# A search that counts against thresholds: the offsets read from PSUM, and the running sum as a fifth column of the digit instruction

## The chip, the cores and the metric

The kernel runs on one core of a Trainium2 chip. The core has five engines with a queue each: PE (TensorE, the matrix products), DVE (VectorE), ACT (ScalarE), POOL (GpSimd) and SP (SyncE, here the queue that starts most DMAs). Each engine works its queue in order; semaphores hold an instruction back until what it needs is there. The metric is the device time of one execution in microseconds, lower is better.

## The reference

An attention part, a mixture of experts, and a second MLP, one after the other:

```python
x = attention(x, state)                       # 4352 tokens of 512 numbers
logits = x @ w_gate                           # 8 experts
order = np.argsort(-logits.flatten())
for idx in order:                             # greedy, best logit first
    tok, e = idx // 8, idx % 8
    if assigned[tok] >= 0 or counts[e] >= 544:
        continue
    assigned[tok] = e
    counts[e] += 1
for e in range(8):                            # each expert has 544 tokens
    h = np.maximum(x[assigned == e] @ w1[e], 0.0)
    out[assigned == e] = h @ w2[e]
h = out @ w_in                                # second MLP
out = np.maximum(0.01 * h, h) @ w_out
```

## The kernel before

It has three stages. `prologue` (0 to about 121 us) does the attention, the logits and the first of seven searches. `experts` (121 to 637 us) runs the eight experts one after the other, in the order in which they fill up, and beside them the other six searches. `mlp2` (to the end) is the second MLP.

**A search** replaces the greedy loop: it finds the expert that fills next, closes it, and leaves its tokens. Its core is `cutoff`, called twice a search (the high 16 bits of the logits, then the low 16): for each expert the 544th largest of 272 numbers in each partition's row `V`, over the rows that belong to that expert. It takes 7 steps. In a step four thresholds are counted: three by DVE (`jD`, line 211, 272 numbers each, `V` minus a running sum, compared with an offset, the count going into `cnt`), the fourth by ACT (`jA`, line 207, with a `bias` that DVE makes on line 200, and a small copy into `cnt`, line 208). PE adds the counts of all rows (`pc`, line 221), and DVE turns them into the next digit (`js`, line 224, whose accumulator output is `acc`). Then DVE's next step begins. Two small instructions behind the counts carry the running sum on: `T` (line 214) and `P` (line 218, the next step's four offsets with `T` added or taken away). At the end one more addition makes the result (`r_hi`, `r_lo`, line 227). So the chain of a step goes DVE, PE, DVE, and one search has 14 of them, and a tail on both engines; `slots` then turns the tokens into gather indices (`u1`, `u2`, `PL`, `rd` on DVE, `pr` on PE, lines 334 to 363).

**An expert** is two products on PE: the first (`pm`, line 872, 192 matmuls in 16 groups of 12) and the second (line 890, 192 matmuls in 8 groups of 24). Every factor is split into a high and a low part, so each group runs three times over its sums. ACT takes each group out of PSUM (lines 878 and 897), and the splits go to ACT (high part) and to POOL or DVE (low part, line 712): weights are `unit`, the hidden layer is `h`. The tokens of the next expert are gathered by POOL's indirect DMAs (`rows`), transposed on PE (`pt`, line 830) and split on ACT and DVE (`xt`, lines 833 and 837). The accumulators `pm` rotate through four PSUM buffers.

**What sets the order.** The program is written out by a small planner. It walks through the matmuls of `ffn`, adds up modelled time, and inserts side work when its time has come: search pieces, slots, weight splits, token transposes. `cutoff` is a generator; each `yield` says how long DVE is expected to take until the next count product, `g.dstep(k)`: 1.95 for k below 2, 2.35 for 2, 2.45 above. So PE's queue holds `pc` at a fixed place among the expert's matmuls: where PE comes to it before the counts are there, PE stands still, since its queue is in order. Experts are numbered 0 to 7 here by their turn; expert k+1 can start only when search k+1 and its slots are done.

These lines are the ones that the prediction's steps touch most:

```python
nc.vector.scalar_tensor_tensor(jD, V, acc, P[:, t:t + 1].to_broadcast([128, 272]), op0=OP.subtract,
                               op1=OP.is_ge, accum_out=cnt[:, t:t + 1])
...
nc.vector.scalar_tensor_tensor(js, pc, float(CAP), C(f"step_{nm}{i}"), op0=OP.is_ge, op1=OP.mult,
                               accum_out=acc)
```

Of the kernel before, what the change touches and what calls it, by code (L numbers as in the profile page):

```python
# [14 lines left out]
OP = mybir.AluOpType  # L15
# [13 lines left out]
MIN_HI = 3.4332275390625e-05  # the high word of 2**-126, read as a float32  # L29
# [4 lines left out]
def _layout_consts():  # L34
# [20 lines left out]
    add("sgn2", np.broadcast_to([1, 1, -1, -1], (128, 4)))  # L55
    add("sgn3", np.broadcast_to([1, 1, 1, -1], (128, 4)))
    add("iota8", np.broadcast_to(np.arange(8), (128, 8)))
    for nm, unit in (("hi", 65536.0), ("lo", 1.0)):
        for i in range(7):
            st = unit * 5.0 ** (6 - i)  # L60
            add(f"step_{nm}{i}", np.broadcast_to([st] * 4, (128, 4)))
            for nd in (2, 3):
                o = [(j + 1) * st if j < nd else 0.5 * unit - (j + 1) * st for j in range(4)]
                add(f"off{nd}_{nm}{i}", np.broadcast_to(o, (128, 4)))
# [29 lines left out]
def setup_select(g):  # L94
# [19 lines left out]
    g.PL = cp.tile([128, 2, 36], F16, name="PL")  # L114
    g.opn = cp.tile([128, E], F32, name="opn")


def load_consts(g, pool):
# [6 lines left out]
    def c(name):  # L125
# [7 lines left out]
        lambda: nc.gpsimd.memset(g.zero, 0.0),  # L133
        lambda: nc.gpsimd.memset(g.opn, 1.0),
        lambda: nc.gpsimd.memset(g.asg, 0.0),
# [1150 lines left out]
```

## Time and profile before

| what | value |
|---|---|
| median of 3 runs | 1423.05 us (1416.94 to 1424.54) |
| the profiled execution's span | 1423.3 us |
| PE busy | 1324.9 us, 93% of the span |
| DVE busy | 737.8 us, 52% |
| ACT, POOL busy | 567.3 us, 505.2 us |
| experts 0 to 7, first matmul to last | about 133 to 637 us |
| second MLP | about 637 to 1423 us |

[...] A matmul's row is longer than the distance to the next one, since matmuls overlap, so PE's idle time is better read from the gaps before a group of instructions than from its busy share.

### The profile page before, as it was taken

The numbers are of one execution on the slowest core, as the hardware profiler recorded it, in microseconds if no ns is written. First come the engines' busy times: TensorE is split into PE (matmuls) and PEld (weight loads), VectorE is DVE, ScalarE is ACT, GpSimd is POOL, SyncE is SP. The second block draws the span as 40 slices with busy tenths as digits, with TensorE's granted clock in tenths as the row PEclk, the third lists the DMA queues.
The fourth block names the chain that finished last, engine by engine and source line by source line (L and its number), as shares of the span: only waits on it lengthen the run. The fifth ranks groups of instructions, "written<-read, shape, count | busy, mean of one in ns | idle before, by whom it ended". The sixth has DMA issues, their size and how long they took to land.

```text
span 1423.3 us, 21798 instructions
## 1 busy us (share of the span) xinstructions
PE 1324.9 (93%) x8145; PEld 1123.0 (79%) x8145; DVE 737.8 (52%) x2071; ACT 567.3 (40%) x1309; POOL 505.2 (35%) x515
## 2 busy tenths in 40 slices
PE   9986678889898999989989999999999999999997
PEld 5564678889888999987668888888888888888886
DVE  6888998998888978557762121121211212112221
ACT  6765645566565646442332222222222222222222
POOL 2303655645546456354543122131221312212121
PEclk9997989999999999999999999999999999999999
DMA  8445050513223377554220000000000000000000
GB/s 344 182 163 210 30 157 26 177 65 123 97 85 125 103 233 247 195 175 138 75 103 30 30 30 30 1 30 30 30 30 1 30 22 30 8 1 30 0 30 15
DMA packets 58746, 123.29 MB, mean 87 GB/s; under 512 B 14992, under 2 KB 24208, under 8 KB 56720
## 3 DMA queue, kind: packets, MB, share of 16 engines
q1 hardware_dynamic: 49504, 102.78, 21.0%
q0 software_dynamic: 5536, 17.83, 3.7%
q10 hardware_dynamic: 3600, 1.29, 0.4%
q8 instruction: 64, 1.05, 0.3%
q14 instruction: 42, 0.34, 0.1%
HBM read 90.94 MB, written 30.93 MB: 86 GB/s over the span
## 4 chain that ended last, share of the span: by engine, by line
PE 70%; DVE 21%; issue 3%; DMA 3%; ACT 3%; POOL 0%; SPq 0%; ACTq 0%; DVEq 0%; POOLq 0%
PE po L1164 24%; PE ph L1147 24%; PE pm L890 7%; PE pm L872 7%; DVE jD L211 6%; PE px L589 2%; DVE bias L200 2%; DVE ot L1015 1%; PE ps L462 1%; DVE P L218 1%; DVE ot L1014 1%; DVE xt L837 1%; DMA rows<-xs,idall 1%; DVE unit L712 1%; DVE T L214 1%
## 5 line engine op out<-in xcount | busy, mean ns | idle before, releaser
L1164 PE MATMUL po<-unit,gt 128*128 128x512 f32 x1632 | 404.4, 396 | 4.9 <-POOL gt L712 4.0
L1164 PEld LDWEIGHTS po<-unit,gt 128*128 128x128 f32 x1632 | 305.5, 188 | 78.5 <-POOL gt L712 6.2
L1151 DVE TENSOR_TENSOR g<-ph,g 128x512 f32<-128x512 f32 (+1 forms) x144 | 95.3, 661 | 511.8 <-ACT g L1150 511.8
L712 POOL TENSOR_TENSOR gt<-g,gt 128x512 fp32r<-128x512 f32 (+1 forms) x80 | 101.9, 1273 | 419.7 <-ACT gt L708 386.9
L1150 ACT ACTIVATE g<-ph 128x512 f32<-128x512 f32 (+1 forms) x144 | 82.4, 572 | 400.4 <-PE ph L1147 400.4
L1147 PE MATMUL ph<-xt,unit 128*128 128x512 f32 (+1 forms) x960 | 215.9, 374 | 8.9 <-ACT unit L708 5.3
L890 PE MATMUL pm<-h,unit 128*128 128x288 f32 (+1 forms) x1536 | 219.6, 301 | 0.0
L872 PE MATMUL pm<-xt,unit 128*128 128x288 f32 (+1 forms) x1536 | 214.4, 296 | 4.3 <-DVE xt L837 2.4
L890 PEld LDWEIGHTS pm<-h,unit 128*128 128x128 f32 x1536 | 207.7, 199 | 0.1
L1147 PEld LDWEIGHTS ph<-xt,unit 128*128 128x128 f32 x960 | 171.8, 191 | 44.1 <-ACT unit L708 5.9
L872 PEld LDWEIGHTS pm<-xt,unit 128*128 128x128 f32 x1536 | 201.7, 193 | 5.3 <-DVE xt L837 2.8
L1147 PE MATMUL ph<-xt_b,unit 128*128 128x512 f32 x768 | 188.4, 394 | 0.0
L1147 PEld LDWEIGHTS ph<-xt_b,unit 128*128 128x128 f32 x768 | 144.0, 188 | 34.2
L712 POOL TENSOR_TENSOR unit<-raw,unit 128x512 fp32r<-128x512 f32 x97 | 128.8, 1340 | 109.9 <-ACT unit L708 109.2
L712 POOL TENSOR_TENSOR h<-h,h 128x288 fp32r<-128x288 f32 (+1 forms) x128 | 109.3, 861 | 88.4 <-ACT h L708 87.3
L211 DVE SCALAR_TENSOR_TENSOR jD<-V,acc,P 128x272 bf16<-128x272 f32 x252 | 139.0, 599 | 0.0
L708 ACT ACTIVATE gt<-g 128x512 fp32r<-128x512 f32 (+1 forms) x144 | 87.6, 608 | 104.8 <-DVE g L1151 104.8
L708 ACT ACTIVATE unit<-raw 128x512 fp32r<-128x512 f32 x144 | 88.2, 620 | 37.3 <-DMA raw<-wf 18.7
L207 ACT ACTIVATE jA<-V,bias 128x272 bf16<-128x272 f32 x84 | 43.8, 521 | 87.8 <-DVE bias L200 86.9
L712 DVE TENSOR_TENSOR gt<-g,gt 128x512 fp32r<-128x512 f32 (+1 forms) x64 | 42.2, 659 | 42.9 <-ACT gt L708 40.0
L878 ACT ACTIVATE h<-pm 128x288 f32<-128x288 f32 (+1 forms) x128 | 49.5, 386 | 35.4 <-PE pm L872 30.1
L712 DVE TENSOR_TENSOR unit<-raw,unit 128x512 fp32r<-128x512 f32 x47 | 39.5, 847 | 40.0 <-ACT unit L708 37.0
(212 smaller groups left out, 1240.1 us busy)
## 6 DMA issues: line engine op xcount, KB each, us to landing
raw<-in_w_dram SPq DMA_DIRECT2D x64, 512.0 KB, 4.3
unit<-in_x_dram SPq DMA_DIRECT2D x8, 1024.0 KB, 12.0
xs<-raw SPq DMA_DIRECT2D x16, 512.0 KB, 2.6
x<-xo SPq DMA_DIRECT2D x64, 128.0 KB, 2.7
raw<-in_win_dram SPq DMA_DIRECT2D x16, 512.0 KB, 3.7
raw<-in_wout_dram SPq DMA_DIRECT2D x16, 512.0 KB, 3.3
raw<-x SPq DMA_DIRECT2D x16, 512.0 KB, 4.4
unit<-in_xT_dram SPq DMA_DIRECT2D x7, 1024.0 KB, 9.9
```

The source lines that it names most:

```text
L200: nc.vector.scalar_tensor_tensor(bias, acc.to_broadcast([128, 4 - nd]), -1.0, P[:, nd:4], op0=OP.mult, op1=OP.add)
L207: nc.scalar.activation(jA, V, AF.Sign, bias=bias[:, t - nd:t - nd + 1], accum_out=cs[:, t - nd:t - nd + 1])
L211: nc.vector.scalar_tensor_tensor(jD, V, acc, P[:, t:t + 1].to_broadcast([128, 272]), op0=OP.subtract, op1=OP.is_ge, accum_out=cnt[:, t:t + 1])
L708: nc.scalar.activation(hi, src, AF.Copy)
L712: e.tensor_tensor(lo, src, hi.bitcast(F32), op=OP.subtract)
L872: nc.tensor.matmul(pm, w[:, a, c, wc], xt[k][:, b, c, o], start=(n == 0), stop=(n == 11))
L878: nc.scalar.activation(h32, pm, AF.Relu)
L890: nc.tensor.matmul(pm, w[:, a, c % 4, 128 * m:128 * m + 128], hs[half][:, b, c, :], start=(n == 0), stop=(n == 23))
L1147: nc.tensor.matmul(ph[:, :n], w[:, a, c, wc], xt[:, b, c, :n], start=(i == 0), stop=(i == 11))
L1150: nc.scalar.activation(g32[:, :n], ph[:, :n], AF.Copy, scale=0.01)
L1151: nc.vector.tensor_tensor(g32[:, :n], ph[:, :n], g32[:, :n], op=OP.max)
L1164: nc.tensor.matmul(pos[gi][t], gt[:, a, 128 * t:128 * t + 128], w[:, b, f % 4, :], start=(f == 0 and a + b == 0), stop=(f == NF - 1 and a ...
```

## The change

The offsets of all 14 steps become one constant row, `offs`, with the sign already in it, and do not depend on the running sum any more. `setup_select` makes a small table `stp` with a row of five columns for each step: four times the step's size, and the running sum. The digit instruction reads five columns: PE's product has five as well, because `cnt` has a fifth column that always holds 100, so the fifth comparison is always true, and the accumulator output is the old sum plus the new digit. It is written straight into the next row of `stp`. So `T`, `P` and the closing addition are gone. The counts on DVE take the sum as a pointer scalar (as before `acc`) and the offset as the broadcast second tensor; in the first search that offset lies in SBUF, in the six searches beside the experts it lies in PSUM: `g.offp`, copied there once at the start of `experts`. `bias` is now a `tensor_scalar` with one tensor input. To make room for `offp` among the eight PSUM banks, the accumulators `pm` rotate through three buffers, not four. The planner's `g.dstep` is 2.15 for all searches. Comments and docstrings are gone, which moves line numbers.

```diff
-    T, acc, P = g.zero, g.zero, C(f"off{nd}_{nm}0")
+    T = None
     for i in range(7):
-        cnt = cp.tile([128, 4], F16, name="cnt", bufs=2)
-        if i:
-            nc.vector.scalar_tensor_tensor(bias, acc.to_broadcast([128, 4 - nd]), -1.0, P[:, nd:4], op0=OP.mult,
-                                           op1=OP.add)
+        n = i if nm == "hi" else 7 + i
+        cnt = g.cnts[n % 2]
+        off = C("offs")[:, 4 * n:4 * n + 4]
+        offv = off if g.offp is None else g.offp[:, 4 * n:4 * n + 4]
+        if T is not None:
+            nc.vector.tensor_scalar(bias, off[:, ND:4], T, None, op0=OP.add)
...
-            nc.vector.scalar_tensor_tensor(jD, V, acc, P[:, t:t + 1].to_broadcast([128, 272]), op0=OP.subtract,
+            nc.vector.scalar_tensor_tensor(jD, V, g.zero if T is None else T,
+                                           offv[:, t:t + 1].to_broadcast([128, 272]), op0=OP.subtract,
                                            op1=OP.is_ge, accum_out=cnt[:, t:t + 1])
-        T2 = cp.tile([128, 1], F32, name="T", bufs=3)
-        nc.vector.tensor_tensor(T2, T, acc, op=OP.add)
-        T = T2
-        if i < 6:
-            P = cp.tile([128, 4], F32, name="P", bufs=2)
-            nc.vector.scalar_tensor_tensor(P, C(f"sgn{nd}"), T, C(f"off{nd}_{nm}{i + 1}"), op0=OP.mult, op1=OP.add)
...
-        nc.vector.scalar_tensor_tensor(js, pc, float(CAP), C(f"step_{nm}{i}"), op0=OP.is_ge, op1=OP.mult,
-                                       accum_out=acc)
-    r = cp.tile([128, 1], F32, name=f"r_{nm}", bufs=2)
-    nc.vector.tensor_tensor(r, T, acc, op=OP.add)
+        T = g.stp[:, n + 1, 4:5] if i < 6 else cp.tile([128, 1], F32, name=f"r_{nm}", bufs=2)
+        nc.vector.scalar_tensor_tensor(js, pc, float(CAP), g.stp[:, n, :], op0=OP.is_ge, op1=OP.mult,
+                                       accum_out=T)
...
-                pm = g.psa.tile([128, HMAX], F32, name="pm", tag="mm", bufs=4)[:, :H]
+                pm = g.psa.tile([128, HMAX], F32, name="pm", tag="mm", bufs=3)[:, :H]
...
-        g.dstep = lambda k: 1.95 if k < 2 else 2.35 if k < 3 else 2.45
+        g.dstep = lambda k: 2.15
...
+            g.offp = g.psa.tile([128, 56], F32, name="offp")
+            nc.vector.tensor_copy(g.offp, g.C("offs"))
```

Three places show what this does to the queues. The first is DVE's queue in a step of the search beside expert 0 (low half). Before:

```order
L224 SCALAR_TENSOR_TENSOR js,acc<-pc,cst 128x4
L200 SCALAR_TENSOR_TENSOR bias<-acc,P 128x1
L211 SCALAR_TENSOR_TENSOR jD_2532,cnt<-V_2416,acc,P 128x272
L211 SCALAR_TENSOR_TENSOR jD_2534,cnt<-V_2416,acc,P 128x272
L211 SCALAR_TENSOR_TENSOR jD_2536,cnt<-V_2416,acc,P 128x272
L214 TENSOR_TENSOR T<-T,acc 128x1
L218 SCALAR_TENSOR_TENSOR P<-cst,T 128x4
L224 SCALAR_TENSOR_TENSOR js,acc<-pc,cst 128x4
```

and now:

```order
L225 SCALAR_TENSOR_TENSOR js,stp<-pc,stp 128x5
L206 TENSOR_SCALAR bias<-cst,stp 128x1
L217 SCALAR_TENSOR_TENSOR jD_2423,cnt_111<-V_2316,stp,offp 128x272
L217 SCALAR_TENSOR_TENSOR jD_2425,cnt_111<-V_2316,stp,offp 128x272
L217 SCALAR_TENSOR_TENSOR jD_2427,cnt_111<-V_2316,stp,offp 128x272
L225 SCALAR_TENSOR_TENSOR js,stp<-pc,stp 128x5
```

Between two `js` stood six instructions, each with two tensor inputs in SBUF. Four are left: `bias` with one tensor input, and three counts with one input in SBUF (`V`) and one in PSUM (`offp`).

The second is PE's queue in the last steps of the search beside experts 2 and 3, where the first product of expert 3 runs. Before:

```order
L221 MATMUL pc<-cnt,m_104 128x4
L872 MATMUL pm<-xt,unit 128x256 x24
L221 LDWEIGHTS m_104
L221 MATMUL pc<-cnt,m_104 128x4
L872 MATMUL pm<-xt,unit 128x256 x22
L221 LDWEIGHTS m_104
L221 MATMUL pc<-cnt,m_104 128x4
L872 MATMUL pm<-xt,unit 128x256 x2
L872 MATMUL pm<-xt,unit 128x288 x18
L221 LDWEIGHTS m_104
```

and now:

```order
L222 MATMUL pc<-cnt_111,m_104 128x5
L871 MATMUL pm<-xt,unit 128x256 x21
L222 LDWEIGHTS m_104
L222 MATMUL pc<-cnt_110,m_104 128x5
L871 MATMUL pm<-xt,unit 128x256 x19
L222 LDWEIGHTS m_104
L222 MATMUL pc<-cnt_111,m_104 128x5
L871 MATMUL pm<-xt,unit 128x256 x10
```

Between two count products `pc` (`m_104` is their constant matrix) stood 20 to 24 matmuls of the expert; now 19 to 21 stand there.

The third is PE's queue where expert 0 ends (line 890 before, 889 now) and expert 1 starts (872, 871), with the token transposes `pt` of expert 1. Before, from the second of its transposes on:

```order
L830 MATMUL pt_3265<-ident,rows 128x128 x4
L890 MATMUL pm<-h_2499,unit 128x288 x7
L221 LDWEIGHTS m_104
L221 MATMUL pc<-cnt,m_104 128x4
L890 MATMUL pm<-h_2499,unit 128x288 x12
L872 MATMUL pm<-xt,unit 128x256 x3
L830 MATMUL pt_3328<-ident,rows 128x128 x4
L872 MATMUL pm<-xt,unit 128x256 x10
L221 LDWEIGHTS m_104
```

and now, from the first on:

```order
L829 MATMUL pt_3070<-ident,rows 128x128 x4
L889 MATMUL pm<-h_2357,unit 128x288 x4
L222 LDWEIGHTS m_104
L222 MATMUL pc<-cnt_110,m_104 128x5
L889 MATMUL pm<-h_2357,unit 128x288 x2
L829 MATMUL pt_3110<-ident,rows 128x128 x4
L871 MATMUL pm<-xt,unit 128x256 x28
L222 LDWEIGHTS m_104
L222 MATMUL pc<-cnt_111,m_104 128x5
L871 MATMUL pm<-xt,unit 128x256 x13
```

The second transpose of expert 1 stood 19 matmuls ahead of the expert's first one; now it stands right in front of it.

## Rows read from the trace of the kernel before

**Rows 1.** The page: busy us of each engine (share); PE's granted clock in tenths, 40 slices.

```profile
PE 1324.9 (93%) x8145; PEld 1123.0 (79%) x8145; DVE 737.8 (52%) x2071; ACT 567.3 (40%) x1309; POOL 505.2 (35%) x515
...
PEclk9997989999999999999999999999999999999999
```

**Rows 2.** Busy time by stretch: experts 0, 1, 4, 7; expert 0's first product.

```profile
core 0: us, PE busy (x) PEld busy (x) DVE busy (x) ACT busy (x) POOL busy (x), PEclk, DMA share, GB/s
...
133.00:218.00 85.00, 64.32 (x441) 59.88 (x442) 76.29 (x268) 44.17 (x126) 47.91 (x45) 0.87 0.31 96
218.00:283.00 65.00, 56.33 (x447) 53.02 (x446) 59.18 (x219) 38.09 (x109) 40.26 (x38) 1.00 0.33 105
...
411.00:472.00 61.00, 56.77 (x443) 54.77 (x442) 53.44 (x215) 37.22 (x105) 33.18 (x35) 0.94 0.35 107
...
586.00:637.00 51.00, 48.65 (x387) 48.22 (x385) 29.41 (x32) 23.57 (x55) 28.57 (x25) 1.00 0.66 209
...
133.00:180.00 47.00, 34.03 (x216) 30.95 (x217) 43.37 (x148) 28.33 (x83) 27.92 (x27) 0.87 0.15 50
```

**Rows 3.** Groups (busy us, mean ns, idle before): whole run; expert 0; a wait at 126-133.

```profile
L200 DVE SCALAR_TENSOR_TENSOR bias<-acc,P 128x1 f32<-128x1 f32 x84 | 38.9, 463 | 5.6
...
L221 PE MATMUL pc<-cnt,m 128*128 128x4 f16 x98 | 17.6, 179 | 38.3 <-DVE jD L211 32.8 <-ACT h L708 2.3 <-ACT unit L708 1.6
L351 PE MATMUL pr<-PL,u 128*128 128x36 f16 x40 | 4.1, 182 | 8.9 <-DVE PL L346 8.9
...
L221 PE MATMUL pc<-cnt,m 128*128 128x4 f16 x20 | 3.7, 184 | 22.1 <-DVE jD L211 21.9 <-ACT unit L708 0.2
...
PE pc L221 <- DVE jD L211: 3.0, 1, 3.0
```

**Rows 4.** DVE by line: duration in ns min/median/max, first and last start.

```profile
L211 DVE SCALAR_TENSOR_TENSOR jD<-V,acc,P x252: 486/495/7095, 84.2 to 484.9; 128x272 bf16<-128x272 f32 x126
...
L200 DVE SCALAR_TENSOR_TENSOR bias<-acc,P x84: 158/160/2941, 84.2 to 483.2; 128x1 f32<-128x1 f32 x84
...
L214 DVE TENSOR_TENSOR T<-T,acc x84: 143/152/1243, 85.5 to 485.3; 128x1 f32<-128x1 f32 x84
...
L262 DVE TENSOR_TENSOR V<-pm,KH x7: 440/441/442, 81.8 to 433.0; 128x272 f32<-128x272 f32 x7
...
L251 DVE TENSOR_TENSOR mk<-L,mg x7: 429/433/441, 79.1 to 432.0; 128x272 bf16<-128x272 f32 x7
...
L837 DVE TENSOR_TENSOR xt<-pt,xt x40: 277/683/691, 128.0 to 579.5; 128x512 fp32r<-128x512 f32 x32, 128x128 fp32r<-128x128 f32 x8
...
L340 DVE TENSOR_SCALAR ce<-tot,ce x8: 212/214/215, 117.9 to 498.7; 128x1 f32<-128x1 f16 x8
...
L346 DVE TENSOR_SCALAR PL<-sc,ce x8: 229/236/1235, 118.7 to 499.8; 128x34 f16<-128x34 f32 x8
...
L358 DVE TENSOR_TENSOR rd<-rr,cst x8: 329/1188/1457, 120.0 to 501.4; 128x170 f32<-128x170 f32 x8
```

**Rows 5.** Timeline, expert 0's second product: start, us, engine, instruction.

```profile
202.45 7.09 DVE L211 SCALAR_TENSOR_TENSOR jD<-V,acc,P 128x272 bf16<-128x272 f32 x1
...
203.08 6.16 POOL L712 TENSOR_TENSOR unit<-raw,unit 128x512 fp32r<-128x512 f32 x5
...
210.46 0.19 PE L221 MATMUL pc<-cnt,m 128*128 128x4 f16 x1 [6.01 <-DVE jD L211]
```

**Rows 6.** Timeline, first search: two digit instructions on DVE; POOL's first work behind it.

```profile
107.71 0.16 DVE L224 SCALAR_TENSOR_TENSOR js<-pc,cst 128x4 f32<-128x4 f32 x1
...
109.69 0.16 DVE L224 SCALAR_TENSOR_TENSOR js<-pc,cst 128x4 f32<-128x4 f32 x1
...
121.06 0.18 POOL L365 COPY idt<-idall 32x1 int32<-32x1 int32 x1 [54.07 <-DVE idall L363]
```

**Rows 7.** Timeline of PE where expert 7 starts.

```profile
586.13 5.77 PE L872 MATMUL pm<-xt,unit 128*128 128x256 f32 x48
593.84 4.43 PE L872 MATMUL pm<-xt,unit 128*128 128x256 f32 x35 [1.94 <-ACT h L878]
```

More of the change, by code (lines that the diff above doesn't have):

```diff
@@ L28 @@
 BIG = 1.0e36
+ND = 3
 MIN_HI = 3.4332275390625e-05
@@ L54, in _layout_consts @@
     add("erev", 8 - p % 8)
-    add("sgn2", np.broadcast_to([1, 1, -1, -1], (128, 4)))
-    add("sgn3", np.broadcast_to([1, 1, 1, -1], (128, 4)))
     add("iota8", np.broadcast_to(np.arange(8), (128, 8)))
-    for nm, unit in (("hi", 65536.0), ("lo", 1.0)):
+    steps, offs = [], []
+    for unit in (65536.0, 1.0):
         for i in range(7):
             st = unit * 5.0 ** (6 - i)
[L61 to L64, printed above, removed]
+            steps += [st] * 4 + [0.0]
+            offs += [(j + 1) * st - (0.0 if j < ND else 0.5 * unit) for j in range(4)]
+    add("steps", np.broadcast_to(steps, (128, 70)))
+    add("offs", np.broadcast_to(offs, (128, 56)))
     _CONST["_n"] = (0, sum(c.shape[1] for c in cols))
@@ L114, in setup_select @@
     g.PL = cp.tile([128, 2, 36], F16, name="PL")
+    g.stp = cp.tile([128, 14, 5], F32, name="stp")
+    g.cnts = [cp.tile([128, 5], F16, name=f"cnt{i}") for i in range(2)]
     g.opn = cp.tile([128, E], F32, name="opn")
@@ L132, in load_consts @@
         lambda: nc.gpsimd.memset(g.ones, 1.0),
-        lambda: nc.gpsimd.memset(g.zero, 0.0),
+        lambda: [nc.gpsimd.memset(g.zero, 0.0)] + [nc.gpsimd.memset(c, 100.0) for c in g.cnts],
         lambda: nc.gpsimd.memset(g.opn, 1.0),
-        lambda: nc.gpsimd.memset(g.asg, 0.0),
+        lambda: [nc.gpsimd.memset(g.asg, 0.0), nc.gpsimd.tensor_copy(g.stp.rearrange("p i t -> p (i t)"), C("steps"))],
         lambda: nc.gpsimd.memset(g.neg16, -1.0),
@@ L188, in keys, with cutoff @@
     return [turn, copy, sign, order, low, high, low_out, high_out]
-def cutoff(g, k, nm, V, nd):
+def cutoff(g, k, nm, V):
     nc, cp, C = g.nc, g.cp, g.C
-    T, acc, P = g.zero, g.zero, C(f"off{nd}_{nm}0")
+    T = None
     for i in range(7):
-        cnt = cp.tile([128, 4], F16, name="cnt", bufs=2)
-        if i:
-            bias = cp.tile([128, 2], F32, name="bias", bufs=2)[:, :4 - nd]
-            nc.vector.scalar_tensor_tensor(bias, acc.to_broadcast([128, 4 - nd]), -1.0, P[:, nd:4], op0=OP.mult,
-                                           op1=OP.add)
+        n = i if nm == "hi" else 7 + i
[3 more added lines that the diff above has]
+        if T is not None:
+            bias = cp.tile([128, 2], F32, name="bias", bufs=2)[:, :4 - ND]
+            nc.vector.tensor_scalar(bias, off[:, ND:4], T, None, op0=OP.add)
@@ L202, in cutoff @@
         else:
-            bias = P[:, nd:4]
+            bias = off[:, ND:4]
         cs = cp.tile([128, 2], F32, name="cs", bufs=2)
-        for t in range(nd, 4):
+        for t in range(ND, 4):
             jA = cp.tile([128, 272], BF16, name="jA")
-            nc.scalar.activation(jA, V, AF.Sign, bias=bias[:, t - nd:t - nd + 1], accum_out=cs[:, t - nd:t - nd + 1])
-        nc.scalar.activation(cnt[:, nd:4], cs[:, :4 - nd], AF.Copy, scale=0.5, bias=136.0)
-        for t in range(nd):
+            nc.scalar.activation(jA, V, AF.Sign, bias=bias[:, t - ND:t - ND + 1], scale=-1.0,
+                                 accum_out=cs[:, t - ND:t - ND + 1])
@@ L210, in cutoff @@
+        nc.scalar.activation(cnt[:, ND:4], cs[:, :4 - ND], AF.Copy, scale=-0.5, bias=136.0)
+        for t in range(ND):
             jD = cp.tile([128, 272], BF16, name=f"jD{t}")
-            nc.vector.scalar_tensor_tensor(jD, V, acc, P[:, t:t + 1].to_broadcast([128, 272]), op0=OP.subtract,
+            nc.vector.scalar_tensor_tensor(jD, V, g.zero if T is None else T,
+                                           offv[:, t:t + 1].to_broadcast([128, 272]), op0=OP.subtract,
                                            op1=OP.is_ge, accum_out=cnt[:, t:t + 1])
-        T2 = cp.tile([128, 1], F32, name="T", bufs=3)
@@ L231, in first_max @@
+    g.res[nm] = T
 def first_max(g):
@@ L233, in first_max, with search @@
     nc.vector.tensor_reduce(g.mg, g.L, axis=AX.X, op=OP.max)
-def search(g, k, nd=3):
+def search(g, k):
     nc, cp, C = g.nc, g.cp, g.C
@@ L262, in search @@
     nc.vector.tensor_tensor(V1, pm, g.KH, op=OP.mult)
-    yield from cutoff(g, k, "hi", V1, nd)
+    yield from cutoff(g, k, "hi", V1)
     Hs = g.res["hi"]
@@ L266, in search @@
     nc.vector.scalar_tensor_tensor(V2, V1, Hs, g.KL, op0=OP.subtract, op1=OP.add)
-    yield from cutoff(g, k, "lo", V2, nd)
+    yield from cutoff(g, k, "lo", V2)
     Lo = g.res["lo"]
@@ L689, in prologue @@
         bg = xread()
-        se = search(g, 0, g.nd0)
+        se = search(g, 0)
         next(bg)
@@ L884, in ffn @@
             for m in range(4):
-                pm = g.psa.tile([128, HMAX], F32, name="pm", tag="mm", bufs=4)[:, :H]
+                pm = g.psa.tile([128, HMAX], F32, name="pm", tag="mm", bufs=3)[:, :H]
                 n = 0
@@ L1213, in moe_kernel @@
         setup_select(g)
-        g.nd0 = 3
+        g.offp = None
         g.gate0 = 4
```

6 lines of the change are left out of this document (2 added, 4 removed).

## The prediction

> **What bounds the kernel now.** I read the page first, then busy time by expert, then what PE waits for, then DVE's durations by line. PE is busy for 93% of the span [rows 1], so a gain must come from gaps on PE or from its clock. Those are in the experts. Expert 7, which has no search beside it, takes 51 us; experts 1 and 4 take 65 and 61, and expert 0 takes 85 [rows 2]. Some of the difference is work (token transposes, count products), but the largest gap is at `pc`: PE stands still for 38.3 us in front of the 98 count products, 22.1 of it in expert 0, and 3.0 in the opening [rows 3], which leaves 13.2 for experts 1 to 5. The releaser is nearly always `jD`, the last count on DVE.
>
> Why DVE is late is seen in its durations. The counts take 495 ns in the middle case and up to 7095; `bias` 160 and up to 2941; `T` 152 and 1243 [rows 4], and `P` is alike. Work of a fixed size should not spread like that. The worst count ran from 202.45 for 7.09 us, and beside it POOL did five splits back to back, 6.16 us; the count ended when they did, and PE waited 6.01 us [rows 5]. All four kinds read two tensors from SBUF. Instructions of the same engine with one tensor in PSUM do not spread: `V` 440 to 442 ns in 7, and `xt` with a middle of 683 and an end of 691 [rows 4]. So a DVE instruction with two SBUF inputs waits for POOL's splits, and one with a PSUM input does not. In the first search, before which and beside which POOL had nothing to do for 54 us, a step takes 1.98 us [rows 6].
>
> **Durations of the new step.** `T` and `P` lay behind the counts and beside the round trip through PE; where nothing stalls they cost nothing, and removing them gives nothing. The counts keep their form except for the PSUM input: `V` with PSUM takes 441 ns and `mk` with two SBUF inputs 433 [rows 4], so I add 0.01 us for each of three. `bias` becomes a `tensor_scalar` with a pointer; `ce` has that form, 214 ns against 160 [rows 4], 0.05 us more. So 1.98 becomes 2.06 us, with or without POOL at work. PE's queue now has 19 to 21 matmuls between two `pc`; 48 took 5.77 us [rows 7], 0.12 each, so 2.3 to 2.5 us, and about the same where they are wider and fewer. DVE is ready before PE arrives, with some 0.25 us to spare.
>
> **Opening** (126 to 133 us). The 3.0 us wait hangs on one `bias` that took 2.94 us. Of it 0.5 is left, since DVE still needs 2.06 us there: **-2.5**.
>
> **Expert 0, first product.** 47 us now, of which ACT is busy 28.3, POOL 27.9 [rows 2], and the 192 matmuls at 0.12 to 0.13 us need 24. With the waits of this half (22.1 less the one of 6.01 [rows 5] and, estimated, one more in the second product) gone, PE would need 32 plus what the opening steps with their token splits still cost, some 3. The three engines then want nearly the same time and feed each other, so I take 35: **-12**.
>
> **Expert 0, second product.** 38 us now; the waits of about 7 go for the most part, DVE's steps still meet `PL`, `u2` and `rd` of the slots, which keep their stalls (`rd` 329 to 1457, `PL` 229 to 1235 [rows 4]). **-6**.
>
> **Experts 1 to 5.** Of 13.2 us at `pc` I leave 7. In each search two steps still hold a slot instruction that waits for POOL: `rd` with about 0.9 us over its shortest, `PL` and `u2` with one us together, and the spacing between two `pc` is now shorter than the 20 to 24 matmuls of before. **-6**. PE also waits 8.9 us for `PL` in front of `pr` [rows 3]. `PL` stands in DVE's queue behind the stalled counts, `T` and `P` of that step; without those it comes on time in about two of three cases, since its own stall stays: **-6**.
>
> **The clock.** PE's granted clock was 0.87 over expert 0 and 0.94 over expert 4, against 1.00 in experts 1 and 7 [rows 2]. It is at the lower of its two levels for 12% of expert 4, so 3.7 us are lost there; experts 2 to 5 together lose perhaps 10. The low stretches come behind gaps of PE. With half of the gaps gone I take half: **-5** (expert 0's share is in its own sums).
>
> **What it costs.** Three accumulators: where expert 7 starts, PE ran four groups (48 matmuls) and then stood 1.94 us until ACT took the first one out [rows 7]. With three buffers it stops 12 matmuls earlier and goes on at the same time, so 1.44 us more; a place or two like it: **+2.5**. Token transposes: the second one of expert 1 now stands right in front of its first matmul. ACT and DVE must split it first, and DVE's split alone is 0.68 us [rows 4]: **+2**. Prologue: 12 steps with a dearer `bias`, less two additions: **+0.3**. The copy of `offp` falls where DVE waits for weights.
>
> Sum: -2.5 - 12 - 6 - 6 - 6 - 5 + 2.5 + 2 + 0.3 = -32.7. The profiled span is 1423.3 us and the median of the runs 1423.05, so the two stand alike, and I forecast **1391 us**. Behind expert 7 nothing changes: the second MLP starts when the experts end.
>
> **Rivals.** *Bias still waits.* `PL` is a `tensor_scalar` with one SBUF input, and it does spread, 229 to 1235 ns [rows 4]. If the new `bias` did so too, some waits would stay: its mean of 463 ns [rows 3] is 0.3 over its shortest, in 72 steps 22 us of DVE time, of which steps with 0.25 us to spare pass on about half: +11, **1402**. Against it stands `ce`, of exactly the new form with one element in a partition, 212 to 215 in 8 [rows 4]. [...]
>
> *ACT takes over.* When DVE is quick, ACT has to serve fourth counts, evictions, hidden splits and weights at PE's pace. In expert 0's first product it is busy 28.3 of 47 us; at 35 us that is 81%. If it falls behind, counts come late from ACT, and three accumulators make each late eviction a gap sooner. Then about half of the gain stays away: **1408**.
>
> *The PSUM input does not free the counts.* Then only `bias`, `T` and `P` are freed; the counts' share of the stalls stays (I take half; the largest one is theirs [rows 5]), and the tighter spacing makes PE wait for it: about **1415**.
>
> *Slower.* The counts read an offset with step 0 from PSUM, which no row shows. If that made each count dearer, the 0.25 us to spare would be used up at 0.08 us a count. Beyond it each of 72 steps passes on three times the excess. To eat up 33 us and lose 8 more it needs 0.08 + 41 / 216 = 0.27 us a count, 0.7 where there is 0.44 now: **1431**. `V` against `mk` speaks against it. [...] The two rows show 0.01.
>
> **How the numbers follow.** The forecast has 0.68; bias 0.07; ACT 0.13; counts not freed 0.05; slower 0.04; 0.03 for no change at all. The forecast's own range goes from 1375, if the waits at `pc` and `pr` and the low clock go almost wholly (3 + 22 + 13 + 7 and some 15 of clock are at most 60), to 1403. The range that holds 8 in 10 takes in the ACT case: 1375 to 1412. About 0.5% (7 us) is what a measurement of this kernel can tell from no change. Faster by more than that: forecast, bias, ACT and half of counts not freed, 0.90; within it 0.06; slower 0.04.
>
> **What would show it.** Right: the counts and `bias` have a maximum near their middle value; PE's wait at `pc` falls from 38 to about 12 us; expert 0 takes some 67 us and not 85; experts 1 to 4 come under 61; the clock shows fewer low stretches. Wrong: counts that still spread; ACT in place of DVE as releaser of `pc`; waits of the first product for `h` on ACT well over 3 us; an expert 0 bound by POOL's weight splits.

## The result and the profile after

The changed kernel takes 1380.85 us (median of 4 runs, 1379.41 to 1383.90) against 1422.86 us (median of 4 as well), a ratio of 0.971 with a 95% interval of 0.969 to 0.973: 42 us faster, where 1391 was forecast. Its profiled execution, the fastest of the four, spans 1377.6 us, 45.7 less than before; the steps below are counted on this pair.

The page, as in [rows 1]:

```profile
PE 1311.3 (95%) x8145; PEld 1110.9 (81%) x8145; DVE 643.6 (47%) x1878; ACT 566.4 (41%) x1309; POOL 498.3 (36%) x516
...
PEclk9997999999999999999999999999999999999999
```

DVE lost 94 us of busy time, far more than the 193 instructions that went: at their undisturbed lengths in [rows 4], with 0.22 us for a `P`, these make an estimated 36 us. The rest was never work, as DVE's durations by line show (ns min/median/max; the answer to [rows 4]):

```profile
L217 DVE SCALAR_TENSOR_TENSOR jD<-V,stp,offp x216: 485/492/501, 130.3 to 425.7; 128x272 bf16<-128x272 f32 x108
...
L206 DVE TENSOR_SCALAR bias<-cst,stp x84: 212/214/216, 85.1 to 424.8; 128x1 f32<-128x1 f32 x84
...
L261 DVE TENSOR_TENSOR V<-pm,KH x7: 408/442/444, 82.8 to 382.1; 128x272 f32<-128x272 f32 x7
...
L265 DVE SCALAR_TENSOR_TENSOR V<-V,r_hi,KL x7: 502/504/2744, 98.6 to 401.9; 128x272 f32<-128x272 f32 x7
...
L345 DVE TENSOR_SCALAR PL<-sc,ce x8: 229/238/1258, 120.0 to 439.3; 128x34 f16<-128x34 f32 x8
```

The counts' longest went from 7095 ns to 501, that of `bias` from 2941 to 216. What still spreads is what the change left alone: `V` on line 265, which reads two tensors from SBUF, and `PL`.

The groups of PE that wait, over the whole run (busy us, mean ns, idle before), beside [rows 3]: 38.3 us became 11.4 at `pc`, and 8.9 became 4.5 at the first `pr`. Expert 0's 22.1 became 1.1 (last line, 131.6 to 194.7 us). The 22.1 hold the 3.0 of the opening too, because that `pc` starts at 133.11 us, just inside the window and just ahead of the expert's first matmul at 133.20; expert 0 itself had 19.2:

```profile
L222 PE MATMUL pc<-cnt,m 128*128 128x5 f16 x98 | 17.6, 179 | 11.4 <-DVE jD L217 10.2 <-ACT unit L707 0.6 <-ACT cnt L214 0.2
L350 PE MATMUL pr<-PL,u 128*128 128x36 f16 x40 | 3.9, 180 | 4.5 <-DVE PL L345 4.4
...
L222 PE MATMUL pc<-cnt,m 128*128 128x5 f16 x20 | 3.6, 180 | 1.1 <-DVE jD L217 0.7 <-ACT cnt L214 0.2
```

Busy time by stretch for experts 0, 1, 4, 7 and expert 0's first product, as in [rows 2]:

```profile
core 0: us, PE busy (x) PEld busy (x) DVE busy (x) ACT busy (x) POOL busy (x), PEclk, DMA share, GB/s
131.60:194.70 63.10, 57.16 (x442) 54.16 (x441) 48.25 (x233) 43.44 (x128) 44.52 (x45) 0.96 0.42 127
194.70:258.30 63.60, 58.98 (x444) 56.58 (x445) 45.78 (x199) 39.15 (x113) 40.97 (x41) 0.93 0.38 117
374.40:434.60 60.20, 55.17 (x449) 52.85 (x448) 47.97 (x220) 36.44 (x103) 32.59 (x34) 1.00 0.34 108
539.80:594.30 54.50, 50.30 (x387) 49.86 (x387) 16.69 (x18) 26.39 (x60) 29.58 (x27) 0.97 0.49 156
131.60:161.20 29.60, 29.09 (x212) 27.56 (x212) 20.75 (x107) 26.56 (x79) 27.06 (x29) 0.92 0.28 90
```

From the first matmul of each product, the time went as follows (us; experts 1 to 5 from start to start, expert 7 to the end of its last matmul):

| stretch | before | after | difference | forecast |
|---|---|---|---|---|
| up to expert 0 | 133.2 | 131.8 | -1.4 | -2.2 |
| expert 0, first product | 46.7 | 29.6 | -17.1 | -12 |
| expert 0, second product | 38.2 | 29.6 | -8.6 | -6 |
| PE waits in front of expert 1 | 0 | 3.9 | +3.9 | +2 |
| experts 1 to 5 | 313.5 | 294.2 | -19.3 | -17 |
| expert 6 | 54.6 | 51.0 | -3.5 | 0 |
| expert 7 | 50.5 | 54.5 | +4.1 | +2.5 |
| second MLP, with the wait in front of it | 786.7 | 783.0 | -3.8 | 0 |

The new wait in front of expert 1 tells where the old mechanism still lives. The timeline (start, us, engine, instruction, [idle before]):

```profile
187.95 4.96 POOL L711 TENSOR_TENSOR unit<-raw,unit 128x512 fp32r<-128x512 f32 x4
...
190.91 2.31 DVE L265 SCALAR_TENSOR_TENSOR V<-V,r_hi,KL 128x272 f32<-128x272 f32 x1
...
193.25 0.52 ACT L212 ACTIVATE jA<-V,cst 128x272 bf16<-128x272 f32 x1 [2.18 <-DVE V L265]
...
194.29 0.59 ACT L832 ACTIVATE xt<-pt 128x512 fp32r<-128x512 f32 x1
...
194.94 1.50 PE L871 MATMUL pm<-xt,unit 128*128 128x256 f32 x5 [3.46 <-ACT xt L832]
```

`V` meets the last two of four splits of POOL in a row and takes 2.31 us in place of 0.50. ACT's count `jA` waits for `V`, the token split `xt` stands behind it in ACT's queue, and PE needs `xt` at once, because the second transpose is now right in front of expert 1's first matmul.

### The profile page after: what moved, and what is told of

Read it like the earlier page. It is cut to its first block, busy times and chain, and to the rows that moved or that the text cites. A ratio compares the mean times of both kernels' runs of the same rounds, so it can differ in the third digit from the quotient of the medians.

```text
span 1377.6 us, 21608 instructions
## 1 busy us (share of the span) xinstructions
PE 1311.3 (95%) x8145; PEld 1110.9 (81%) x8145; DVE 643.6 (47%) x1878; ACT 566.4 (41%) x1309; POOL 498.3 (36%) x516
## 4 chain that ended last, share of the span: by engine, by line
PE 50%; DVE 4%; issue 1%; ACT 1%; DMA 0%; POOL 0%; SPq 0%; POOLq 0%; ACTq 0%; DVEq 0%
PE po L1163 25%; PE ph L1146 25%; DVE ot L1014 1%; DVE ot L1013 1%; DVE ot L1012 1%; DVE ot L1016 1%; ACT g L1149 0%; DVE ot L1015 0%; DMA x2t<-xo 0%; ACT unit L707 0%; ACT xt_b L707 0%; POOL out_dram L1128 0%; DVE g L1150 0%; ACT xo L896 0%; ACT xt L707 0%
## 5 line engine op out<-in xcount | busy, mean ns | idle before, releaser
L889 PE MATMUL pm<-h,unit 128*128 128x288 f32 (+1 forms) x1536 | 209.6, 293 | 0.4 <-ACT h L877 0.4
L1146 PEld LDWEIGHTS ph<-xt,unit 128*128 128x128 f32 x960 | 170.4, 189 | 40.5 <-ACT unit L707 5.9
L889 PEld LDWEIGHTS pm<-h,unit 128*128 128x128 f32 x1536 | 197.8, 191 | 1.1 <-ACT h L877 0.7
L711 POOL TENSOR_TENSOR unit<-raw,unit 128x512 fp32r<-128x512 f32 x95 | 126.0, 1333 | 80.5 <-ACT unit L707 78.9
L217 DVE SCALAR_TENSOR_TENSOR jD<-V,stp,offp 128x272 bf16<-128x272 f32 x216 | 95.4, 491 | 0.2 <-issue 0.2
L711 DVE TENSOR_TENSOR unit<-raw,unit 128x512 fp32r<-128x512 f32 x49 | 43.2, 884 | 70.3 <-ACT unit L707 55.1
```

Source lines behind the costliest of these rows:

```text
L217: nc.vector.scalar_tensor_tensor(jD, V, g.zero if T is None else T, offv[:, t:t + 1].to_broadcast([128, 272]), op0=OP.subtract, op1=OP.is_ ...
L711: e.tensor_tensor(lo, src, hi.bitcast(F32), op=OP.subtract)
L889: nc.tensor.matmul(pm, w[:, a, c % 4, 128 * m:128 * m + 128], hs[half][:, b, c, :], start=(n == 0), stop=(n == 23))
L1146: nc.tensor.matmul(ph[:, :n], w[:, a, c, wc], xt[:, b, c, :n], start=(i == 0), stop=(i == 11))
```

## The experiments

The first theory: DVE instructions with two SBUF inputs wait for POOL's splits, and the change takes counts, `bias`, `T` and `P` out of that. Rivals: the gain comes from the shorter chain (fewer instructions), from the new spacing of the count products, or from the placement that three accumulators bring. Ratios are to the kernel before, run again beside each (medians of 1422.3 to 1424.7 us), with 95% intervals.

**The counts' offsets back in SBUF.** All else as after.

```diff
             nc.vector.tensor_copy(g.offp, g.C("offs"))
+            g.offp = None
```

> The changed kernel, but the counts in all searches read their offsets from the constants in SBUF; the three accumulators, the digit instruction and the spacing stay. If the PSUM operand frees the counts from POOL (theory A), they spread again (a maximum over 1 us where the changed kernel has 501 ns), PE's wait in front of the count products rises from 11.4 to 20 us or more, and the time is 1395 to 1410 us. If the gain comes from the small instructions that are gone or made cheap (theory B), the time stays under 1388 us. If it comes from the planner's new spacing (theory C), it stays at 1381.

Measured: 1422.73 us, 1.000 (0.999 to 1.002). The whole gain is gone, more than expected. Durations of the counts (ns min/median/max):

```profile
L217 DVE SCALAR_TENSOR_TENSOR jD<-V,stp,cst x252: 490/498/4179, 84.1 to 467.3; 128x272 bf16<-128x272 f32 x126
```

The median is 498 ns against 492 from PSUM: reading the offset from PSUM costs nothing and takes the tail away. PE's wait at `pc` goes from 11.4 to 40.5 us. The tail lies where POOL works: with the 42 counts of the first steps there are 294 counts in a run; 77 took over 600 ns here, and each of these overlapped a `tensor_tensor` on POOL (of the other 217, 29 did). In after 158 of the 294 did, and none took over 502 ns. With the same instructions and queues otherwise, 42 us hang on where this operand lies, so neither the shorter chain nor the spacing made them by itself.

**The offsets alone in PSUM**, in the kernel before: each step's `P` is written to a PSUM tile (three accumulators make the room).

```diff
-            P = cp.tile([128, 4], F32, name="P", bufs=2)
+            P = cp.tile([128, 4], F32, name="P", bufs=2) if g.Pp is None else g.Pp[:, i % 2, :]
```

> The kernel before, with one part of the change: the offsets P of each step are written to PSUM and read there by the counts and by bias (so both have one SBUF input); T, P and the closing addition stay, with two SBUF inputs; three accumulators, the old spacing. Theory A: the counts and bias no longer spread, T and P still do, and the time falls to 1393 to 1405 us. Theory B: T and P still delay slots and steps, and the time stays within 8 us of 1423. Theory C: 1423.

Measured: 1396.95 us, 0.982 (0.979 to 0.985), as the theory said. The counts from this tile:

```profile
L211 DVE SCALAR_TENSOR_TENSOR jD<-V,acc,Pp x216: 489/493/500, 128.7 to 455.7; 128x272 bf16<-128x272 f32 x108
```

`T` is still there with two SBUF inputs, and so is `P`, whose own inputs are the constants and `T`, as is the old chain of instructions. `bias`, whose `P` now lies in PSUM too, took 154 to 160 ns. What still reads two SBUF tensors stalls as before or longer:

```profile
L218 DVE SCALAR_TENSOR_TENSOR Pp<-cst,T x72: 229/231/5644, 126.5 to 453.5; 128x4 f32<-128x4 f32 x72
```

So a chain of the old length with its operand moved gives 26 us. After gains 42, and 53 at the spacing of this run (below).

**The digit instruction alone**: after, offsets in SBUF, spacing of before.

```diff
-        g.dstep = lambda k: 2.15
+        g.dstep = lambda k: 1.95 if k < 2 else 2.35 if k < 3 else 2.45
...
+            g.offp = None
```

> The changed kernel with the counts' offsets in SBUF and the old spacing (1.95, 2.35, 2.45), three accumulators: the digit instruction and the new bias alone, against the kernel before. The run with the new spacing showed 1422.7, and the spacing alone cost the kernel before 22.6 us. If the two only add, this one comes to 1400 us, with counts that still spread over 1 us. If the digit instruction brings nothing as long as the counts stall, 1415 to 1424.

Measured: 1407.61 us, 0.989 (0.987 to 0.991), between the two cases of the forecast. Dropping `T` and `P` and freeing `bias` is worth 1.1% even with counts that stall up to 6586 ns. And beside the first experiment, which differs in the spacing alone, the wider spacing is worth 15 us when counts stall. So the 42 us of that experiment hold a part of the spacing's price; at the old spacing the place of the offsets is worth 38 us (this run against 1369.40 below).

**Three accumulators alone**, in the kernel before.

```diff
-                pm = g.psa.tile([128, HMAX], F32, name="pm", tag="mm", bufs=4)[:, :H]
+                pm = g.psa.tile([128, HMAX], F32, name="pm", tag="mm", bufs=3)[:, :H]
```

> The kernel before with three accumulators and nothing else: the price of the freed PSUM bank. By the trace of before 1.4 us where expert 7 starts and about 1 us in other places: 1424 to 1428 us. The changed kernel's expert 7 took 4 us longer than before; if all of that is the third buffer's absence, 1427 or more.

Measured: 1423.21 us, 1.000 (0.998 to 1.002). In the whole time no price can be told. Where expert 7 starts the trace, of an execution of 1431.20 us, shows one all the same: PE ran 36 matmuls and stood 4.20 us, where it had run 48 and stood 1.94 [rows 7].

**`bias` with two SBUF inputs again**, else as after.

```diff
-            nc.vector.tensor_scalar(bias, off[:, ND:4], T, None, op0=OP.add)
+            nc.vector.scalar_tensor_tensor(bias, T.to_broadcast([128, 4 - ND]), 1.0, off[:, ND:4], op0=OP.mult,
+                                           op1=OP.add)
```

> The changed kernel with bias in its old form, two SBUF inputs (the sum times one, plus the offset). It stalls again behind POOL, up to 3 us, mean stall 0.3 us, and heads the step's chain: 72 steps give 22 us of DVE, of which 6 to 15 reach PE: 1387 to 1396 us. If bias does not matter because the spacing has room, 1381 to 1384.

Measured: 1398.50 us, 0.983 (0.981 to 0.985), 18 us slower than after, somewhat more than expected:

```profile
L206 DVE SCALAR_TENSOR_TENSOR bias<-stp,cst x84: 158/162/4289, 84.0 to 443.2; 128x1 f32<-128x1 f32 x84
...
L223 PE MATMUL pc<-cnt,m 128*128 128x5 f16 x98 | 17.7, 181 | 21.5 <-DVE jD L218 14.8 <-ACT unit L708 4.9 <-ACT raw L591 0.7
```

The form that is quicker undisturbed, 162 ns against 214, is the dearer one in the kernel, with the same mean as in [rows 3], 463 ns.

**`T` and `P` put back** as work that nobody reads, each with two SBUF inputs, behind the counts of after.

```diff
+        T2 = cp.tile([128, 1], F32, name="T", bufs=3)
+        nc.vector.tensor_tensor(T2, g.zero, g.zero if T is None else T, op=OP.add)
+        if i < 6:
+            P = cp.tile([128, 4], F32, name="P", bufs=2)
+            nc.vector.scalar_tensor_tensor(P, C("iota8")[:, :4], T2, off, op0=OP.mult, op1=OP.add)
```

> The changed kernel with T and P put back behind the counts as work that nobody reads, with two SBUF inputs each. They lie beside PE's round trip, so they cost nothing unless they stall; by the trace of before they stalled 0.11 us each in the mean, and held up the slot instructions behind them. Theory: 3 to 10 us more than 1381, PE's waits in front of pr back near 9 us. If the digit instruction's gain lies elsewhere: 1381.

Measured: 1405.58 us, 0.988 (0.986 to 0.990), 25 us slower than after: a clear miss of the size. PE's wait in front of `pr` came back as said (10.1 us), but that at `pc` rose too, from 11.4 to 18.4. `T` alone ranged up to 4052 ns and averaged 294, `P` 393. They lie beside the round trip through PE only as long as they don't stall; where they do, the digit instruction, and with it the next step, comes late:

```profile
L221 DVE TENSOR_TENSOR T<-zero,stp x84: 149/154/4052, 85.7 to 450.7; 128x1 f32<-128x1 f32 x84
...
L224 DVE SCALAR_TENSOR_TENSOR P<-cst,T 128x4 f32<-128x4 f32 x84 | 33.0, 393 | 3.0
```

**The new spacing alone**, in the kernel before.

```diff
-        g.dstep = lambda k: 1.95 if k < 2 else 2.35 if k < 3 else 2.45
+        g.dstep = lambda k: 2.15
```

> The kernel before with the planner's spacing of 2.15 for all searches and nothing else. Theory C: most of the gain, 1385 to 1400 us. Theories A and B: with stalled counts PE comes to the count products earlier and waits more in experts 2 to 5, less in expert 0; 1415 to 1432 us, no gain that can be told from none.

Measured: 1445.14 us, 1.016 (1.013 to 1.019). The spacing is no cause of the gain; with counts that stall it costs 23 us, more than expected.

**The old spacing in the kernel after**, the reverse of that edit.

> The changed kernel with the old spacing. With free counts a step takes 2.06 us, under every spacing but that of the searches beside expert 0 (1.95, about 2.0 us on PE); so the spacing should matter little: 1378 to 1387 us, with 1 to 3 us more waits in expert 0, later searches, and the tokens of expert 1 earlier. If the new spacing were worth as much with free counts as it costs with stalled ones, 1360 or 1400.

Measured: 1369.40 us, 0.962 (0.960 to 0.964), 11.5 us better than after. The forecast held that the shorter spacing is free, so it fell here. With this run the parts also stand side by side at the old spacing: PSUM alone 1.8% (`bias` is freed there too), digit instruction and `bias` alone 1.1%, both 3.8%. Together they give more than the sum, as they would if a step that is late through one stalled instruction gains little from freeing another; that reason is argued, not measured.

**The old value for the first two steps only.**

```diff
-        g.dstep = lambda k: 2.15
+        g.dstep = lambda k: 1.95 if k < 2 else 2.15
```

> The changed kernel with the old spacing of 1.95 for the search beside expert 0 alone; the others keep 2.15. It asks where the 11.5 us lie by which the old spacing is better. If they come from the tokens of expert 1, whose transposes the later search pushes right in front of its first matmul (PE lost 4 us there), this run gets back 4 to 6 us: 1375 to 1377. If they come from the tighter steps of experts 1 to 4, where slot instructions lie between the counts, it stays at 1379 to 1383.

Measured: 1379.53 us, 0.970 (0.967 to 0.974), the same as after. Expert 0 became 2 us shorter and expert 1's tokens were in time, yet PE's wait at `pc` did not fall: 14.9 us against 11.4, the longest of them 5.1 us in expert 3. So the price lies in the later steps.

**A spacing a little wider than before's.**

```diff
-        g.dstep = lambda k: 1.95 if k < 2 else 2.35 if k < 3 else 2.45
+        g.dstep = lambda k: 1.95 if k < 2 else 2.45 if k < 3 else 2.55
```

> The kernel after with a spacing a little wider than that of before: 1.95, then 2.45 for the third step and 2.55 for the later ones (before's spacing gave 1369.4 us, 2.15 gave 1380.9). If the room between two count products is what costs at 2.15, the curve must flatten here: in the run with before's spacing PE's waits at pc were down to 3.8 us, of which at most 2 can still go, and 10 steps of a search get 0.1 us longer, so each of five searches ends 1 us later: 1366 to 1374. If wider is better for another reason (side work that falls elsewhere), it goes on falling: under 1364. If 1369 was a lucky place of the side work rather than the room, it goes back towards 1380: over 1376.

Measured: 1383.55 us, 0.972 (0.968 to 0.975), back where after is. The room alone was to give 1366 to 1374; by the forecast's words this is the case in which the old spacing had a lucky place of the side work. Room at `pc` is thus one side only. PE's idle time in experts 1 to 5, by the groups of that stretch (us):

| spacing from the fourth step on | at `pc` | at `pr` | at transposes | at the first product |
|---|---|---|---|---|
| 2.15 (after) | 7.6 | 4.7 | 0.5 | 5.2 |
| 2.45 (of before) | 1.7 | 5.4 | 2.7 | 1.0 |
| 2.55 | 0.0 | 0.4 | 3.5 | 8.5 |

At 2.55 the search ends so late that in front of each of experts 2 to 5 the second transpose stands right before the first matmul, and PE waits for its tokens to be split. The timeline at expert 5, wide spacing first, then PE's at the same place with before's:

```profile
421.04 0.60 PE L829 MATMUL pt<-ident,rows 128*128 128x128 f32 x4
...
422.54 0.39 ACT L896 ACTIVATE xo<-pm 128x288 f32<-128x288 f32 x1
422.83 0.59 ACT L832 ACTIVATE xt<-pt 128x512 fp32r<-128x512 f32 x1
...
423.47 4.51 PE L871 MATMUL pm<-xt,unit 128*128 128x256 f32 x33 [1.83 <-ACT xo L896]
```

```profile
414.74 0.60 PE L829 MATMUL pt<-ident,rows 128*128 128x128 f32 x4
415.10 1.57 PE L889 MATMUL pm<-h,unit 128*128 128x288 f32 x10
416.50 1.70 PE L871 MATMUL pm<-xt,unit 128*128 128x256 f32 x13
```

The row names `xo` as the releaser, but `xo` ends at 422.93 us, 0.5 us too early; what ends just before PE goes on is the split `xt`, at 423.42. Ten matmuls between the two make the wait vanish. Of the 12.2 us by which the wide run's profile is longer (1380.4 against 1368.2), experts 1 to 5 hold 8.3, by their starts; 3.2 lie in PE's wait in front of the second MLP, 6.38 us against 3.21, of which more below.

**Four accumulators**, with the old spacing; the room comes from the transposes' second buffer.

```diff
-            pt = g.psa.tile([128, 4, 128], F32, name="pt4", tag="tx", bufs=2)
+            pt = g.psa.tile([128, 4, 128], F32, name="pt4", tag="tx", bufs=1)
...
-                pm = g.psa.tile([128, HMAX], F32, name="pm", tag="mm", bufs=3)[:, :H]
+                pm = g.psa.tile([128, HMAX], F32, name="pm", tag="mm", bufs=4)[:, :H]
```

> The changed kernel with the old spacing and four accumulators; the bank is taken from the token transposes, which get one PSUM buffer and not two. Expert 7's first product goes back to about 26 us; if the third buffer costs only there, 1365 plus what the single transpose buffer costs in the opening, some 1 to 4 us: 1365 to 1371.

Measured: 1397.52 us, 0.981 (0.977 to 0.985), 28 us slower than three with two and far off the forecast. PE waits at the transposes now, 31.9 us against 5.7:

```profile
L829 PE MATMUL pt<-ident,rows 128*128 128x128 f32 (+1 forms) x152 | 24.7, 289 | 31.9 <-DVE xt L836 15.8 <-issue 14.6 <-DMA rows<-xs,idall 1.5
```

Expert 7's start tells about the accumulators: with a fourth buffer PE ran 48 matmuls instead of 36 before it stopped. It then stood 4.22 us all the same, because the DMA that ACT waits for there came later: 8.44 us of waiting against 7.01 with three buffers (over the whole run 20.0 against 18.6).

**Second-MLP weights ahead of expert 7**, with the old spacing. In after, ACT's queue at that place is the reason (timeline; `raw<-wf` is the load of those weights):

```profile
540.15 4.42 PE L871 MATMUL pm<-xt,unit 128*128 128x256 f32 x36
540.40 0.41 ACT L896 ACTIVATE xo<-pm 128x288 f32<-128x288 f32 x1 [2.76 <-PE pm L889]
547.09 0.63 ACT L707 ACTIVATE unit<-raw 128x512 fp32r<-128x512 f32 x1 [6.28 <-DMA raw<-wf]
547.63 0.36 ACT L877 ACTIVATE h<-pm 128x256 f32<-128x256 f32 x1
...
548.04 4.24 PE L871 MATMUL pm<-xt,unit 128*128 128x256 f32 x24 [3.47 <-ACT h L877]
```

ACT holds its queue for a DMA, 6.28 us, and the eviction that PE waits for stands behind it. The edit starts the loads sooner and plans the splits later:

```diff
-                sch.add(g.t0 + 1.0 + 2.7 * n, g.w_next)
+                sch.add(g.t0 + 6.0 + 2.0 * n, g.w_next)
...
+        if n + 2 < W_EARLY:
+            load(n + 2)
...
+    load(0)
```

> The changed kernel with the old spacing, and where expert 7 starts the first weights of the second MLP are asked for at once and split from 6 us of planned time on, each later pair one pair ahead. It removes ACT's wait for that DMA in front of the first evictions. If the 4 us that expert 7 costs more with three accumulators come from that wait, its first product goes from 30 to about 26 us and the time from 1369.4 to 1364 to 1367. If they come from three buffers in general, 1369.

Measured: 1359.48 us, 0.956 (0.953 to 0.959), the best of all, 21 us under after and 10 under the old spacing alone, more than forecast. In the pair of profiles expert 7 gives 6.0 us of that and expert 0 another 3.1, at a granted clock of 0.97 for 0.91 (131 to 190 us), for which the edit gives no reason. Expert 7's first product runs without a gap, 24.3 us where the old spacing alone had 30.1:

```profile
521.51 24.32 PE L871 MATMUL pm<-xt,unit 128*128 128x256 f32 x192
```

## Why the prediction was right, and which of its steps were not

**The cause holds.** The counts with two SBUF inputs took up to 7095 ns; from PSUM they run 485 to 501 ns, and moving the offsets back costs all 42 us (38 at the old spacing). That POOL is what they wait for rests on the overlap counted above and on [rows 5] and [rows 6]; no run takes POOL's splits away. The rival that the PSUM input does not free them is out, and so is the slower one: a count from PSUM with step 0 was to cost up to 0.27 us more and costs nothing, 492 ns against 495. The rival that `bias` still waits is out too: 212 to 216 ns in 84, of which 47 overlapped a `tensor_tensor` on POOL.

**The new step** was to take 2.06 us; three digit instructions of the first search, whose offsets still lie in SBUF and beside which POOL has no work, stand 2.03 us apart:

```profile
108.91 0.17 DVE L225 SCALAR_TENSOR_TENSOR js<-pc,stp 128x5 f32<-128x5 f32 x1 [0.28 <-PE pc L222]
...
110.94 0.16 DVE L225 SCALAR_TENSOR_TENSOR js<-pc,stp 128x5 f32<-128x5 f32 x1 [0.27 <-PE pc L222]
...
112.96 0.17 DVE L225 SCALAR_TENSOR_TENSOR js<-pc,stp 128x5 f32<-128x5 f32 x1 [0.27 <-PE pc L222]
```

**The opening** lost its whole wait of 2.95 us, and the first search, from its first count product to its first `pr`, took 0.3 us longer, as forecast. But that first product already comes 0.95 us later than before (84.68 for 83.73 us), for which no run gives the reason.

**Expert 0** was undersized, -25.7 for -18. I took 35 us for its first product because three engines want nearly the same time; it took 29.6, with ACT at 26.56 and POOL at 27.06 us of it, some 90% each. Engines that busy did not hold PE back here, and ACT did not take over: its counts held `pc` for 0.2 us. The waits I had counted too high: the 3.0 us of the opening stand in the 22.1 as well, so the first product had 12.6 us of them and not 15. And I had given the expert's clock no term of its own. The granted clock (the share of full speed that PE was given) rose from 0.87 to 0.96 over the whole expert. PE's pace goes with it: in before 12 matmuls of 128x288 took 3.23 us at 0.50 (from 210.51 us), and 18 took 2.63 at 1.00 (from 198.92). What it lacks to 1.00, times the length, is my estimate of the time lost: 11.0 us before and 2.5 after. Of the 11.0 some 2.0 cost nothing, since PE stood still at `pc` for 4 us of the lower clock (before; columns as in [rows 2]):

```profile
206.40:210.40 4.00, 0.00 (x0) 0.00 (x0) 4.00 (x7) 0.00 (x0) 3.83 (x4) 0.50 0.89 234
```

So some 6.5 of the 25.7 us that both products lost are the clock's, and 18 the waits' at `pc` (19.2 to 1.0). What the sum missed, 7.7 us, is about the clock's part.

**Experts 1 to 5** came out near, -19.3 against -17, by other shares. At `pc` 13.3 us became 7.6 in that stretch, -5.7 where I said -6. At `pr`, both lines, 8.7 became 4.7: -4 for -6. The clock: over experts 1 to 5 the granted clock times their lengths gives 10.7 us lost before and 5.1 after (expert 1 at 0.93, expert 2 at 0.99, the others at 1.00), -5.6 for -5; this is the most it can be, since PE stood still in some of it. The remaining 4 us I had not seen: PE's waits at the token transposes, for gathered rows (2.6 to 0.5), and at `pb`, a small product of the slots that waits for DVE (1.9 to 0). Expert 1 kept 63.6 us where I said under 61: its clock fell to 0.93.

**The step that failed is "some 0.25 us to spare".** I compared the step's own chain, 2.06 us, with the matmuls between two `pc`, and called the tighter spacing free. It costs 11.5 us here. In the two profiles (1377.6 and 1368.2 us) experts 1 to 5 are 10.5 us longer with it, of which 5.9 are waits at `pc` (1.7 to 7.6) and some 3 the clock's share as above. DVE's queue between two counts holds more than the chain. The two longest waits at `pc` beside the experts in after show it, each with what made DVE late:

```profile
300.82 2.51 POOL L711 TENSOR_TENSOR unit<-raw,unit 128x512 fp32r<-128x512 f32 x2
300.90 2.74 DVE L265 SCALAR_TENSOR_TENSOR V<-V,r_hi,KL 128x272 f32<-128x272 f32 x1
...
305.08 0.18 PE L222 MATMUL pc<-cnt,m 128*128 128x5 f16 x1 [1.93 <-DVE jD L217]
...
406.80 0.62 ACT L707 ACTIVATE unit<-raw 128x512 fp32r<-128x512 f32 x1
...
407.51 2.01 DVE L711 TENSOR_TENSOR unit<-raw,unit 128x512 fp32r<-128x512 f32 x1 [3.74 <-POOL h L711]
...
409.44 0.15 DVE L225 SCALAR_TENSOR_TENSOR js<-pc,stp 128x5 f32<-128x5 f32 x1
...
411.16 0.18 PE L222 MATMUL pc<-cnt,m 128*128 128x5 f16 x1 [2.94 <-DVE jD L217]
```

The first is `V` between the two halves of a search, with two SBUF inputs: 2.74 us where 0.50 is the middle. The second is a weight split on DVE in front of the digit instruction, and only part of it is a stall: 2.01 us where the same split at 252.46 us takes 0.69. Before that DVE's queue stood 3.74 us, of which 2.1 lie behind the count product at 405.18 (0.17 us), whose sums the digit instruction needs. The row names POOL, but what ends just before the split starts is ACT's high part of the same weights, at 407.42. So 4 us went by between that product and the digit instruction, 1.3 of them by the stall. The next longest, 1.78 us at 255.39, has no stall at all: two splits, one of which waited 1.36 us for ACT, stood in front of the digit instruction. My figure left out both, the side work in the queue and what that work waits for. "Nothing" for `T` and `P` failed by the stalls: undisturbed they lie beside the round trip, with POOL at work they cost 25 us when put back.

**What it costs.** Expert 1's late tokens were right in place and half in size, 3.9 for 2: I counted DVE's split and not `V`, through ACT. For three accumulators the mechanism held and the size was low, +4.1 for +2.5. PE stopped 12 matmuls earlier and stood 3.47 us in place of 1.94, 1.53 more where 1.44 was forecast; another 0.7 us of waits in that product and a granted clock of 0.97 where it was 1.00 (1.7 us) I had not seen. The number of buffers sets when PE stops there. When it goes on is set by ACT's wait for a DMA, and without that wait the gap is gone with three buffers too.

**What I gave as zero.** Expert 6 gained 3.5 us: 1.9 in PE's waits (2.5, at token transposes, to 0.6), and some 1.7 of clock (0.97 to 1.00). Behind expert 7 "nothing changes" was wrong. Of the 3.8 us there 3.1 lie in front of the second MLP's first product, where ACT again holds its queue for weights, with the last evictions of expert 7 behind (before, then after):

```profile
637.44 0.63 ACT L708 ACTIVATE unit<-raw 128x512 fp32r<-128x512 f32 x1 [3.57 <-DMA raw<-wf]
...
640.27 4.89 PE L1147 MATMUL ph<-xt,unit 128*128 128x512 f32 x14 [3.68 <-ACT xo L897]
```

```profile
591.44 0.63 ACT L707 ACTIVATE unit<-raw 128x512 fp32r<-128x512 f32 x1 [1.70 <-DMA raw<-wf]
...
595.23 5.06 PE L1146 MATMUL ph<-xt,unit 128*128 128x512 f32 x21 [0.55 <-ACT xo L896]
```

That wait was 3.68 us in before, 0.55 in after, 3.21 at the old spacing and 6.38 at the wide one, by when the DMA lands. So some 3 of the 45.7 us in this pair are luck: where that DMA fell, and not the counts.

## What to carry to other kernels

Where durations of one instruction spread while its size does not, look at what its neighbour engines do at that moment, and at how many of its tensor inputs lie in SBUF; one operand moved to PSUM was worth more here (26 us) than the shorter chain together with a freed `bias` (15 us). Cost a queue of fixed places by all that stands in it and by what that waits for, not by the chain alone, and when the chain gets steadier, time the places again from both sides: too tight and the product waits (7.6 us at `pc` at 2.15), too loose and the next stage's inputs come late (8.5 us at the first product at 2.55). An eviction that the bounding engine waits for should not stand behind an instruction that waits for a DMA (ACT held its queue 6.28 us for one, and PE stood 3.47).

## What the runs showed of the hardware

- One stall can outlast one neighbour instruction: `V` took 2.74 us beside two splits of POOL that took 2.51, as the count of 7.09 us beside five in [rows 5].
- A `tensor_scalar` on one element a partition never waited, 212 to 216 ns in 84 with 47 of them beside POOL's `tensor_tensor`, while `PL`, the same operation on 34, took 229 to 1258.
- Reading the offset from PSUM as a scalar broadcast over 272 numbers had no price, 489 to 500 ns with 493 in the middle against 495 from SBUF; writing `P` there took 231 ns in the middle case against 223 into SBUF.
